# A delta-rule attention feeding a maxout FFN: when weights are converted, four key-query products made and a triangular substitution run inside the first FFN group

## The chip, the cores and the metric

One core of a Trainium2 chip runs the kernel. The metric is the device time in microseconds. Engines are called by the profile's names: PE (TensorE, with PEld for its weight loads), DVE (VectorE), ACT (ScalarE), POOL (GpSimd), SP (SyncE, which here only issues DMAs).

## The reference

```python
# B, H, S, D = 4, 8, 768, 48; d_model = H*D = 384, d_ff = 768
k_n = k / (norm(k, axis=-1, keepdims=True) + 1e-6)
state = zeros((B, H, D, D))
for t in range(S):
    y[:, :, t] = einsum('bhd,bhde->bhe', q[:, :, t], state)
    v_old = einsum('bhde,bhd->bhe', state, k_n[:, :, t])
    state += beta[:, :, t, None, None] * einsum('bhd,bhe->bhde', k_n[:, :, t], v[:, :, t] - v_old)
x = y.transpose(0, 2, 1, 3).reshape(B * S, H * D)        # 3072 x 384
h = maximum(maximum(x @ w1, x @ w2), x @ w3)             # 3072 x 768
out = h @ w_out                                          # 3072 x 384
```

## The kernel before, in words

The recurrence is taken in chunks of 64 positions: 12 chunks, each of two *units* (a unit is half of the batches), so 24 units. Two chunks make a *group*: six groups, each giving 512 rows of x to the FFN. The program is written out by hand (`manual_schedule`): every engine runs its instructions in program order, and each waits only for what it needs.

For a chunk, `gram` makes the key-key products (`at`) and the key-query products (`pt`, masked on DVE by `masked`) of each unit. `to_dram` writes `at` to a DRAM tile, `blocks(m)` reads a group's `at` back with the layout turned, and `solve(m)` runs a forward substitution on DVE: 31 columns of two instructions (L574 makes `tmp`, L578 subtracts it). It is a generator: one step prepares it (norms, scaling), 31 steps are the columns, one step writes the result to DRAM (`y_d`), and two steps issue four reads each from there into `ut`, for the group's first and second chunk. `some(solving, n)` takes n such steps. Then a chunk goes through a chain that `EARLY_LINKS` names by letters:

- z (`join_z`) and j (`join_u`) join the two 32-row halves of `ut`; d (`turn_t1`) transposes parts of it on DVE for j.
- k (`old_k`) and q (`old_q`) multiply by the state; u (`new`), s (`step`, adds to the state on DVE), y (`to_y`, uses `pt`) and x (`to_x`) follow.
- t (`turn`) and g (`gram`) prepare the units of the group after.

Weights come as fp32 bits: `fetch` issues one DMA of 384 KB for a piece, `weights()` converts it: three ACT multiplications (`mant` and two halves of `up`), and a call later `joined` shifts `mant` on DVE (L254) and adds the two on POOL (L263). There are 24 pieces: 18 of w1, w2, w3 (six column blocks, each of the three matrices), then six rows of w_out. For pieces 13 to 21 the kernel before uses another form, two ACT multiplications and one more DVE instruction (L259) that carries the sign. `some(conv, 1)` is one call.

The part in question is the loop over `ffn(0)`, the FFN of group 0, into which the work of groups 1 and 2 is woven. Its 31 steps are:

- 0 to 17: column blocks 0 to 2 of the hidden layer, for 256 rows (0 to 8), then for the other 256 (9 to 17), one weight matrix a step (three pairs of matmuls, 128x256). The first of three steps is copied to `h` by ACT, the two others are maxima on DVE (L949).
- 18 to 26: column blocks 3 to 5 for all 512 rows.
- 27 to 30: the output products with w_out.

The products `p_h` and `p_o` share two PSUM buffers (tag "ffn"), so a step's products wait for the evacuation of the second-last step. All else in PSUM shares three buffers (tag "two"). `at`, `pt`, `h` and a few more share 17 SBUF buffers (tag "square"). The step's products come first; then in this order: fetches, `queries(FIRST[i])`, `links(1, EARLY_LINKS[i])`, the conversion, the substitution, and the rest of the loop (`blocks(2)` at 18, `less_first`, which subtracts w1 from w2 and w3, `turn_first`, `prep_values`, which scales v on POOL by the key norms from `solve`).

In `FIRST` the names T and P are the queries' turns and the key-query products of units 2 to 7: P4 to P7 are four calls of `gram(n, (1,))`, one for each unit of group 1. S takes steps of the substitution of group 1. x and y of that substitution lie inside `wo_sb`, where w_out goes later.

In the profiled execution, step 6 starts on PE at 76.95 us, step 12 at 94.44, step 18 at 111.67, step 20 at 123.89, step 24 at 146.91 and step 27 at 161.57. The FFN of group 1 starts at 179.80.

Of the kernel before, what the change touches and what calls it, by code (L numbers as in the profile page):

```python
# [9 lines left out]
FP32 = mybir.dt.float32  # L10
# [4 lines left out]
ALU = mybir.AluOpType  # L15
# [8 lines left out]
def kernel(  # L24
# [31 lines left out]
    nc = tc.nc  # L56
# [52 lines left out]
    def rows(bb):  # L109
        return slice(C * bb, C * (bb + 1))  # L110
# [19 lines left out]
    def load_k(n, queues=one_queue):  # L130
        load(k, kpad[place(n)], n, queues)

    def load_q(n, queues=one_queue):
        load(q, qpad[n % NQ], n, queues)

    def load_v(c, queue=nc.sync):
        vts[c] = work.tile([128, 2, H, D], FP32, name="v_t", bufs=3)
        for bb in range(2):
            queue.dma_start(  # L139
                out=vts[c][rows(bb)].rearrange("p g h d -> p (g h) d"),  # L140
                in_=v[2 * bb : 2 * bb + 2, :, c * C : (c + 1) * C, :].rearrange(
                    "b h p d -> p (b h) d"
                ),
            )
# [36 lines left out]
    for bb in range(2):  # L181
        nc.gpsimd.affine_select(
            out=mask[rows(bb)], in_=mask[rows(bb)], pattern=[[1, C]], base=-1,
# [4 lines left out]
    t1 = [const.tile([128, 2, H, BL], FP32, name=f"t1{i}") for i in range(NU)]  # L188
# [7 lines left out]
    pieces = []  # L196
# [14 lines left out]
    def fetch(queue=nc.scalar):  # L211
        if fetched[0] < len(pieces):
            _, src, (a, b) = pieces[fetched[0]]
            st = work.tile([128, 2 * 384], U32, name="w_bits", bufs=5)
            queue.dma_start(
                out=st.rearrange("p (a b) -> p a b", a=a), in_=src
            )
            staged.append(st)
            fetched[0] += 1

    def weights():

        waiting = None
        for n, (dst, _, (a, b)) in enumerate(pieces):
            bits = staged.popleft().rearrange("p (a b two) -> p a b two", a=a, two=2)
            low, high = bits[:, :, :, 0], bits[:, :, :, 1]
            mant = work.tile([128, 384], U32, name="mant", bufs=2)
            up = work.tile([128, 384], I32, name="up", bufs=2)  # L230
            mant_v = mant.rearrange("p (a b) -> p a b", a=a)
            up_v = up.rearrange("p (a b) -> p a b", a=a)
            halves = [
                up.bitcast(t)[:, i::2].rearrange("p (a b) -> p a b", a=a)
                for i, t in enumerate((I16, FP16))
            ]

            nc.scalar.mul(mant_v.bitcast(FP32), high.bitcast(FP32), 2.0**-112)
            if not 13 <= n < 22:
                nc.scalar.mul(halves[0], low, 2.0**-29)  # L240
                nc.scalar.mul(halves[1], high.bitcast(FP32), 2.0**-64)
                high = None
            else:
                nc.scalar.mul(up_v, low, 2.0**-29)
            if waiting:
                joined(*waiting)
            waiting = dst, high, mant, mant_v, up_v
            yield
        joined(*waiting)
        yield  # L250

    def joined(dst, high, mant, mant_v, up_v):

        nc.vector.tensor_scalar(  # L254
            out=mant, in0=mant, scalar1=3, scalar2=None,
            op0=ALU.logical_shift_left,
        )
        if high is not None:
            nc.vector.scalar_tensor_tensor(  # L259
                out=mant_v, in0=high, scalar=0x80000000, in1=mant_v,  # L260
                op0=ALU.bitwise_and, op1=ALU.bitwise_or,
            )
        nc.gpsimd.tensor_tensor(  # L263
            out=dst.bitcast(I32), in0=mant_v.bitcast(I32), in1=up_v, op=ALU.add
        )
# [35 lines left out]
    def prep_values(c):  # L301

        if c in nrms:
            scale(c, nrms.pop(c))
# [41 lines left out]
    kqts, ats, pts, xs, at_d = {}, {}, {}, {}, {}  # L346
# [172 lines left out]
    def blocks(m):  # L519
        if m == 1:  # L520
            xs[m] = in_wo(0)
        else:
            xs[m] = work.tile([128, 2, HB * BL + HB], FP32, name="x_bl", bufs=1)
        nc.sync.dma_start(
            out=in_rows(xs[m]),
            in_=at_d[m].rearrange("c f b h j i -> (c f b h) j i"),
        )
# [99 lines left out]
    def both(name, w, bufs=1):  # L627
        return work.tile([128, 2, H, w], FP32, name=name, bufs=bufs)
# [110 lines left out]
    def heads(t):  # L739
        return t.rearrange("p g (j two) d -> p two (g j) d", two=2)  # L740

    def times_state(kqt, i, name):
        p_b = ps_two(name)
        for j in range(NP):
            for g in range(2):
                for par in range(2):
                    for bb in range(2):
                        c0 = (g * NP + j) * D
                        nc.tensor.matmul(  # L749
                            p_b[rows(bb), par, c0 : c0 + D],  # L750
                            kqt[g][dims(par), j, bb ^ g, i],
                            st[dims(par), bb ^ g, g, j],
                        )
        return p_b[:, :, 0 : H * D].rearrange("p two (x d) -> p two x d", d=D)
# [8 lines left out]
            )  # L763

    def old_q(c):
        kqt = [kqts.pop(2 * c + g) for g in range(2)]
        if c:
            qs = qss[c] = both("qs", D)
            nc.scalar.copy(heads(qs), times_state(kqt, 1, "p_q"))
# [211 lines left out]
    def some(gen, n):  # L981
        for _ in range(n):
            if next(gen, gen) is gen:
                break

    conv = weights()
    solving = solve(0)
    zeros(*(t[:, :, :, D:DP] for t in kmore), qall[:, :, :, D:DP])
# [68 lines left out]
    for c in range(2):  # L1057
# [24 lines left out]
    solving = solve(1)  # L1082
# [9 lines left out]
    }  # L1092
    EARLY_LINKS = {
# [3 lines left out]
    }  # L1097


    FIRST = {  # L1100
        0: "f1 s0 T2 S1 S1", 1: "z1 d1 S1 k1 P2 T3 S1 S1", 2: "j1 S1 S1 S1",
        3: "P3 S1 q1 S1 S1", 4: "u1 T4", 5: "y1", 6: "s1 T5 P4", 7: "x1 T6",
        8: "P5 T7", 10: "P6", 12: "P7",
    }


# [8 lines left out]
    def links(m, names):  # L1115
        for name in names.split():
            f, i = name[0], int(name[1])
            if f in RECURS and m < GROUPS:
                RECURS[f](2 * m + i)
            elif f in MADE and m + 1 < GROUPS:  # L1120
                MADE[f](2 * (m + 1) + i)
            elif f in UNIT and m + 1 < GROUPS:
                UNIT[f](4 * (m + 1) + i)
            elif f == "N" and m + 2 < GROUPS:
                load_blocks(4 * (m + 2) + i)

    def queries(names):
        for name in names.split():
            f, n = name[0], int(name[1])
            if f not in OF_KEYS:  # L1130
                links(0, name)
                continue
            OF_KEYS[f](n)
            if f == "T" and n + 3 < 11:
                load_q(n + 3)

    CONVERTED = {*range(9), 10, *range(12, 24)}
    for i, _ in enumerate(ffn(0)):  # L1140
        if i - 1 in CONVERTED:
            fetch(nc.sync)
        queries(FIRST.get(i, ""))
        links(1, EARLY_LINKS.get(i, ""))
        if i in CONVERTED:
            some(conv, 1)
        if 3 < i < 17:
            some(solving, (2, 1, 1, 1, 2, 2, 2, 2, 2, 2, 3, 2, 1)[i - 4])
        if i in (5, 7):
            prep_values(i // 2)  # L1150
        if i in (1, 7):
            for n in range(2):
                load_k(8 + 2 * (i > 1) + n, (nc.gpsimd, nc.gpsimd))
        if i == 0:
            load_v(3)
        if i == 11:
            load_q(11, (nc.gpsimd, nc.gpsimd))
        if i in (10, 22):
            load_v(4 + i // 22)
        if i == 18:  # L1160
            blocks(2)
        if i == 21:
            solving = solve(2)
            some(solving, 1)
        if i == 22:
            prep_values(4)
        if 21 < i < 27:
            some(solving, 3)
        if i >= 27:
            some(solving, 4 if i < 30 else 5)  # L1170
        if i in (27, 28, 29):
            load_blocks(i - 15, nc.sync)
        if i in (15, 17, 19, 22, 25, 27):
            less_first((15, 17, 19, 22, 25, 27).index(i))
        if 27 <= i < 30:
            turn_first((2 * (i - 27), 2 * (i - 27) + 1))
# [5 lines left out]
    for m in range(1, GROUPS):  # L1182
        for i, _ in enumerate(ffn(m)):
# [4 lines left out]
            if m + 2 < GROUPS:  # L1188
                if i == 6:
                    blocks(m + 2)  # L1190
                if i == 8:
                    solving = solve(m + 2)
# [32 lines left out]
```

## Time and profile before

| what | value |
|---|---|
| median of 8 runs | 538.23 us (534.29 to 541.98) |
| the profiled execution | 537.42 us, span 535.7 us |
| mean granted TensorE clock | 0.954 |
| PE busy | 499.7 us (93%) |
| DVE busy | 315.8 us (59%) |
| ACT busy | 160.0 us (30%) |
| POOL busy | 173.8 us (32%) |

The page's shares are means over stages that differ: the first 80 us or so are attention work before and at the start of the FFN, then the FFN of group 0 with the work of groups 1 and 2 in it, then five more FFN groups. In the slices each digit is a fortieth of the span, 13.4 us, in tenths busy; PEclk is the clock granted to TensorE in the same tenths. In a list of waits a row names the waiting instruction, what it waited for, the total in us, the number of waits and the longest. In a timeline a row gives the start, the duration, engine, line, operation and tiles; an idle time ahead of it stands in brackets.

### The profile page before, as it was taken

Reading aid. Unit: us, or ns where it says so; the run is one execution under the profiler, and the core shown is the slowest. Engines: PE = TensorE matmul, PEld = TensorE weight load, DVE = VectorE, ACT = ScalarE, POOL = GpSimd, SP = SyncE. Lnnn points to the kernel's source line nnn. Section 1 sums busy time; section 2 is a strip of 40 time slices with the busy share of each in tenths; the row PEclk is TensorE's granted clock in tenths of the full one; section 3 lists DMA queues with packets and bytes.
Section 4 is the critical chain, followed back from the end, with each engine's and each line's share of the span. In section 5 each row is a group of like instructions: output and inputs, shape, how many; then the busy total and the mean of one; then the engine's idle time right before and its main releaser. Section 6 shows DMA issues by size and latency. Waiting matters only on the chain.

```text
span 535.7 us, 18031 instructions
## 1 busy us (share of the span) xinstructions
PE 499.7 (93%) x7840; PEld 308.8 (58%) x7840; DVE 315.8 (59%) x704; ACT 160.0 (30%) x294; POOL 173.8 (32%) x289
## 2 busy tenths in 40 slices
PE   6657889968899999999999999999999999999996
PEld 5546768834546555556555565565565555654453
DVE  6885989967779553199763699563988222101100
ACT  5547656536222223210134210143101321011100
POOL 7215246322381191694085890411330000000000
PEclk9656989997989999999999999999999999999999
DMA  8876578674123592544394654554334302130011
GB/s 112 185 164 140 104 192 178 131 152 116 32 70 83 112 187 43 127 128 115 84 180 80 158 144 112 118 90 91 89 76 91 64 2 61 45 75 0 0 27 32
DMA packets 114047, 53.45 MB, mean 100 GB/s; under 512 B 95857, under 2 KB 108497, under 8 KB 113969
## 3 DMA queue, kind: packets, MB, share of 16 engines
q1 hardware_dynamic: 104592, 39.02, 33.9%
q0 software_dynamic: 7264, 12.90, 10.1%
q8 instruction: 61, 1.00, 0.8%
q10 hardware_dynamic: 2112, 0.39, 0.5%
q14 instruction: 18, 0.14, 0.1%
HBM read 39.17 MB, written 13.11 MB: 98 GB/s over the span
## 4 chain that ended last, share of the span: by engine, by line
PE 77%; DVE 13%; ACT 3%; issue 2%; DMA 2%; SPq 1%; POOL 0%; DVEq 0%; ACTq 0%; POOLq 0%
PE p_h L935 33%; PE p_o L967 25%; PE p_g L447 3%; PE p_y L819 2%; PE p_m L915 2%; PE p_u L777 2%; PE p_k L749 2%; DVE tmp L574 2%; PE p_q L749 2%; DVE wo_sb L578 2%; PE p_j L732 2%; PE p_s L800 1%; PE p_z L718 1%; DMA kpad<-in_k_dram 1%; ACT ut L593 1%
## 5 line engine op out<-in xcount | busy, mean ns | idle before, releaser
L935 PE MATMUL p_h<-xt,w_sb 128*128 128x512 f32 (+1 forms) x522 | 221.1, 569 | 3.6 <-DVE h L949 1.5
L935 PEld LDWEIGHTS p_h<-xt,w_sb 128*128 128x128 f32 x522 | 96.6, 194 | 90.8 <-issue 82.7
L967 PE MATMUL p_o<-wo_sb,h 128*128 128x384 f32 x288 | 97.8, 489 | 0.0
L949 DVE TENSOR_TENSOR h<-h,p_h 128x512 f32<-128x512 f32 (+1 forms) x48 | 29.6, 616 | 90.8 <-PE p_h L935 90.8
L967 PEld LDWEIGHTS p_o<-wo_sb,h 128*128 128x128 f32 x288 | 53.7, 190 | 35.7 <-issue 0.5
L574 DVE TENSOR_TENSOR tmp<-x_bl,y_bl 128x31 f32<-128x31 f32 (+20 forms) x139 | 52.9, 380 | 4.2
L973 ACT COPY o_sb<-p_o 128x384 f32<-128x384 f32 x24 | 11.5, 479 | 135.6 <-PE p_o L967 129.6
L578 DVE TENSOR_TENSOR y_bl<-y_bl,tmp 128x31 f32<-128x31 f32 (+20 forms) x139 | 47.4, 341 | 4.8
L945 ACT ACTIVATE h<-p_h 128x512 f32<-128x512 f32 x30 | 17.9, 597 | 87.9 <-PE p_h L935 86.4
L967 PE MATMUL p_o<-w_sb,xt 128*128 128x384 f32 x120 | 42.0, 486 | 0.0
L405 POOL DMA_DIRECT2D turned<-in_q_dram x72 | 39.0, 550 | 4.6 <-POOL turned L400 3.0
L447 PE MATMUL p_g<-kqt 48*64 48x64 f32 (+1 forms) x1216 | 28.4, 243 | 7.8 <-DVE nt_bl L272 4.2
L447 PEld LDWEIGHTS p_g<-kqt 48*64 48x64 f32 x1216 | 25.0, 143 | 15.8 <-ACT kqt L376 7.6
L967 PEld LDWEIGHTS p_o<-w_sb,xt 128*128 128x128 f32 x120 | 22.8, 190 | 15.9
L263 POOL TENSOR_TENSOR w_sb<-mant,up 128x384 int32<-128x384 int32 x18 | 18.4, 1023 | 40.3 <-DVE mant L254 26.9
L431 DVE TENSOR_TENSOR pt<-p_g,mask 128x512 f32<-128x512 f32 x22 | 15.1, 688 | 19.7 <-PE p_g L447 15.2
L120 POOL DMA_DIRECT2D kpad<-in_k_dram x32 | 21.8, 688 | 14.7 <-PE p_s L800 14.7
L296 POOL TENSOR_TENSOR v_t<-v_t,nrm 128x768 f32<-128x768 f32 x12 | 18.1, 1510 | 25.5 <-DVE nrm L275 13.5
L807 DVE TENSOR_TENSOR st<-st,p_s 48x768 f32<-48x768 f32 (+1 forms) x18 | 17.1, 949 | 15.4 <-PE p_s L800 15.2
L400 POOL MEMSET turned<- 128x96 f32 x18 | 3.3, 191 | 62.6 <-DVE kqt L421 40.0
L139 POOL DMA_DIRECT2D v_t<-in_v_dram x12 | 9.9, 827 | 36.8 <-PE p_u L777 18.4
L464 ACT COPY at<-p_g 128x512 f32<-128x512 f32 x21 | 12.3, 585 | 29.2 <-DVE pt L431 26.9
(152 smaller groups left out, 611.5 us busy)
## 6 DMA issues: line engine op xcount, KB each, us to landing
w_bits<-in_moe_w_dram SPq DMA_DIRECT2D x18, 384.0 KB
out_dram<-o_sb SPq DMA_DIRECT2D x48, 96.0 KB
turned<-in_q_dram POOLq DMA_DIRECT2D x72, 48.0 KB, 2.6
kpad<-in_k_dram POOLq DMA_DIRECT2D x32, 96.0 KB, 4.7
y_x<-y SPq DMA_DIRECT2D x16, 192.0 KB
qall<-y_x SPq DMA_DIRECT2D x32, 96.0 KB
at_d<-at SPq DMA_DIRECT2D x80, 32.0 KB
ut<-y_d SPq DMA_DIRECT2D x40, 64.0 KB
```

What stands on the lines that cost most here:

```text
L120: queues[bb].dma_start(out=dst[rows(bb ^ g), :, 0:D], in_=src[2 * bb + g, :, c * C : (c + 1) * C, :].rearrange("h p d -> p h d"),)
L263: nc.gpsimd.tensor_tensor(out=dst.bitcast(I32), in0=mant_v.bitcast(I32), in1=up_v, op=ALU.add)
L296: nc.gpsimd.tensor_tensor(out=vts[c], in0=vts[c], in1=nrm[:, :, :, None].to_broadcast([128, 2, H, D]), op=ALU.mult,)
L405: (queue, nc.gpsimd)[i].dma_start(out=t[p0 : p0 + 32, bb, at : at + NP * 2 * D].rearrange("p (j x) -> p j x", j=NP), in_=(k, q)[i][2 * bb ...
L447: nc.tensor.matmul(p_g[rows(bb ^ (g * i)), par, c0 : c0 + C * (1 + whole)], kq[:, 0], kq if whole else kq[:, i],)
L574: nc.vector.tensor_tensor(out=t_v, in0=row.to_broadcast(t_v.shape), in1=column.to_broadcast(t_v.shape), op=ALU.mult,)
L578: nc.vector.tensor_tensor(out=rest, in0=rest, in1=t_v, op=ALU.subtract)
L749: nc.tensor.matmul(p_b[rows(bb), par, c0 : c0 + D], kqt[g][dims(par), j, bb ^ g, i], st[dims(par), bb ^ g, g, j],)
L935: nc.tensor.matmul(p_h, w_sb[i][:, t, f * 128 : (f + 1) * 128], xt[:, t, lo : lo + w], start=(t == 0), stop=(t == KT - 1),)
L945: nc.scalar.activation(out=h, in_=p_h, func=mybir.ActivationFunctionType.Relu)
L949: nc.vector.tensor_tensor(out=h, in0=h, in1=p_h, op=ALU.max)
L967: nc.tensor.matmul(p_o, stays, moves, start=(n == 0), stop=(n == len(terms) - 1))
```

## The change

- `weights()` and `joined()` lose the second form: all 24 pieces are converted with three ACT multiplications, one DVE shift and one POOL addition.
- The calls of the conversion move: steps 0 to 5, 11 to 17 and 20 to 25 (two calls in 22 and 24) instead of 0 to 8, 10 and 12 to 23. The fetches follow them.
- P4 to P7 move from steps 6, 8, 10 and 12 to 14, 15, 16 and 17.
- The substitution of group 1 takes 2, 1, 2, 2, 3, 3, 3, 3, 2, 2 steps in 4 to 13, instead of 2, 1, 1, 1, 2, 2, 2, 2, 2, 2, 3, 2, 1 in 4 to 16. Its last column falls in step 12 instead of 14, with the writes to `y_d`, and all eight reads in 13; before, the writes and the first four reads were in 15 and the last four in 16.
- The links: g0 in 12 (was 13); z0 and z1 in 18 (19); j0 and j1 in 19 (20); u0 in 20 (21); s0 in 21 (22).
- The substitution of group 2 starts in 22 (21), and `prep_values(4)` goes to 23 (22); later steps take five instead of four of its steps.
- `old_q` reads `kqts` without taking the entry out, since P4 to P7 now come after it.

```diff
             nc.scalar.mul(mant_v.bitcast(FP32), high.bitcast(FP32), 2.0**-112)
-            if not 13 <= n < 22:
-                nc.scalar.mul(halves[0], low, 2.0**-29)
-                nc.scalar.mul(halves[1], high.bitcast(FP32), 2.0**-64)
-                high = None
-            else:
-                nc.scalar.mul(up_v, low, 2.0**-29)
+            nc.scalar.mul(halves[0], low, 2.0**-29)
+            nc.scalar.mul(halves[1], high.bitcast(FP32), 2.0**-64)
...
-        if high is not None:
-            nc.vector.scalar_tensor_tensor(
-                out=mant_v, in0=high, scalar=0x80000000, in1=mant_v,
-                op0=ALU.bitwise_and, op1=ALU.bitwise_or,
-            )
...
-        kqt = [kqts.pop(2 * c + g) for g in range(2)]
+        kqt = [kqts[2 * c + g] for g in range(2)]
...
     EARLY_LINKS = {
-        9: "k0 q0", 10: "t0", 11: "t1", 13: "g0 t2", 14: "g1", 15: "t3", 16: "g2", 17: "g3",
-        18: "d0 d1", 19: "z0 z1", 20: "j0 j1", 21: "u0", 22: "s0", 23: "k1 y0 q1",
-        24: "u1 x0", 25: "s1", 26: "y1", 28: "x1",
+        9: "k0 q0", 10: "t0", 11: "t1", 12: "g0", 13: "t2", 14: "g1", 15: "t3",
+        16: "g2", 17: "g3", 18: "d0 d1 z0 z1", 19: "j0 j1", 20: "u0", 21: "s0",
+        23: "k1 y0 q1", 24: "u1 x0", 25: "s1", 26: "y1", 28: "x1",
     }
     FIRST = {
...
-        3: "P3 S1 q1 S1 S1", 4: "u1 T4", 5: "y1", 6: "s1 T5 P4", 7: "x1 T6",
-        8: "P5 T7", 10: "P6", 12: "P7",
+        3: "P3 S1 q1 S1 S1", 4: "u1 T4", 5: "y1", 6: "s1 T5", 7: "x1 T6",
+        8: "T7", 14: "P4", 15: "P5", 16: "P6", 17: "P7",
     }
...
-    CONVERTED = {*range(9), 10, *range(12, 24)}
+    CONVERTED = {i: 1 + (i in (22, 24)) for i in (*range(6), *range(11, 18), *range(20, 26))}
     for i, _ in enumerate(ffn(0)):
-        if i - 1 in CONVERTED:
+        for _ in range(CONVERTED.get(i - 1, 0)):
             fetch(nc.sync)
...
-        if i in CONVERTED:
-            some(conv, 1)
-        if 3 < i < 17:
-            some(solving, (2, 1, 1, 1, 2, 2, 2, 2, 2, 2, 3, 2, 1)[i - 4])
+        some(conv, CONVERTED.get(i, 0))
+        if 3 < i < 14:
+            some(solving, (2, 1, 2, 2, 3, 3, 3, 3, 2, 2)[i - 4])
...
-        if i == 21:
+        if i == 22:
             solving = solve(2)
             some(solving, 1)
-        if i == 22:
+        if i == 23:
             prep_values(4)
-        if 21 < i < 27:
+        if 22 < i < 27:
             some(solving, 3)
         if i >= 27:
-            some(solving, 4 if i < 30 else 5)
+            some(solving, 5)
```

More of the change, by code (lines that the diff above doesn't have):

```diff
@@ L225, in weights @@
         waiting = None
-        for n, (dst, _, (a, b)) in enumerate(pieces):
+        for dst, _, (a, b) in pieces:
             bits = staged.popleft().rearrange("p (a b two) -> p a b two", a=a, two=2)
@@ L238, in weights @@
             nc.scalar.mul(mant_v.bitcast(FP32), high.bitcast(FP32), 2.0**-112)
-            if not 13 <= n < 22:
-                nc.scalar.mul(halves[0], low, 2.0**-29)
-                nc.scalar.mul(halves[1], high.bitcast(FP32), 2.0**-64)
-                high = None
-            else:
-                nc.scalar.mul(up_v, low, 2.0**-29)
+            nc.scalar.mul(halves[0], low, 2.0**-29)
+            nc.scalar.mul(halves[1], high.bitcast(FP32), 2.0**-64)
             if waiting:
                 joined(*waiting)
-            waiting = dst, high, mant, mant_v, up_v
+            waiting = dst, mant, mant_v, up_v
             yield
@@ L250, in weights, with joined @@
         yield
-    def joined(dst, high, mant, mant_v, up_v):
+    def joined(dst, mant, mant_v, up_v):
         nc.vector.tensor_scalar(
```

## The prediction

> **What bounds the kernel now.** First the page's slices: from the twelfth on (about 147 us) TensorE stands at 9 throughout but for the last, at 6. What comes later is paid for in products; idle time to be won lies earlier.
>
> ```profile
> PE   6657889968899999999999999999999999999996
> DVE  6885989967779553199763699563988222101100
> PEclk9656989997989999999999999999999999999999
> ```
>
> The edit first acts in step 6, whose products start at 76.95 us. So next the waits of TensorE alone from 76 to 165 us: four in all.
>
> ```profile
> PE p_z L718 <- DMA ut<-y_d: 4.1, 1, 4.1
> PE p_k L749 <- DVE st L807: 2.6, 1, 2.6
> PE p_h L935 <- DVE h L949: 1.5, 1, 1.5
> PE p_h L935 <- ACT h L943: 0.8, 1, 0.8
> ```
>
> Then the stages of 5 us (span, PE busy, PE loads, VectorE, ScalarE, GpSimd, clock, DMA): two holes, each followed by a low clock.
>
> ```profile
> 115.00:120.00 5.00, 2.74 (x69) 1.21 (x67) 2.20 (x5) 1.45 (x3) 0.54 (x1) 1.00 0.87 163
> 120.00:125.00 5.00, 2.39 (x66) 1.77 (x67) 4.78 (x10) 1.87 (x5) 0.76 (x2) 0.60 0.82 177
> 125.00:130.00 5.00, 5.00 (x135) 2.58 (x133) 4.65 (x8) 3.41 (x7) 2.06 (x2) 0.71 0.43 144
> 140.00:145.00 5.00, 2.44 (x130) 1.91 (x132) 4.83 (x10) 0.25 (x1) 1.55 (x2) 0.99 0.00 0
> 145.00:150.00 5.00, 5.00 (x80) 3.33 (x74) 4.93 (x9) 0.08 (x1) 4.71 (x10) 0.50 0.17 45
> ```
>
> Last the timeline, which says why the first hole is there.
>
> ```profile
> 100.51 0.32 DVE L578 TENSOR_TENSOR wo_sb<-wo_sb,tmp 128x156 f32<-128x156 f32 x1
> 102.77 1.00 POOL L263 TENSOR_TENSOR w_sb<-mant,up 128x384 int32<-128x384 int32 x1 [2.84 <-DVE mant L259]
> 102.86 1.06 DVE L578 TENSOR_TENSOR wo_sb<-wo_sb,tmp 128x135 f32<-128x135 f32 x1
> 108.39 0.21 DVE L578 TENSOR_TENSOR wo_sb<-wo_sb,tmp 128x31 f32<-128x31 f32 x1
> 109.30 1.16 SPq L600 DMA_DIRECT2D y_d<-wo_sb  x2
> 113.16 1.91 SPq L609 DMA_DIRECT2D ut<-y_d  x4
> 115.70 1.86 SPq L477 DMA_DIRECT2D at_d<-at  x4
> 117.66 2.86 SPq L609 DMA_DIRECT2D ut<-y_d  x4
> 121.85 1.27 PE L718 MATMUL p_z<-ut,at 32*32 32x32 f32 x64 [4.11 <-DMA ut<-y_d]
> ```
>
> Group 1's substitution ends at 108.6, its result is written at 109.30, and the second chunk's reads stand on SP behind four `at_d` writes. So z1 (`join_z` of chunk 3) waits. From 80.9 to 109.3 the chain of waits runs through VectorE nearly alone: its queue sets that end. The two L578 rows around 102 us show one of its loads: a column under a GpSimd addition took 1.06, beside 0.32.
>
> **The change part by part.**
>
> *VectorE ahead of the substitution's end.* The four key-query masks (0.69, the next instruction starting 0.60 to 0.68 later) leave steps 6, 8, 10 and 12: 4 x 0.65 = 2.6. Conversions called before the end fall from 13 to 8 (steps 0-8, 10, 12-14 against 0-5, 11, 12): 5 shifts of about 0.3 make 1.5, and four fewer columns under a GpSimd addition, 0.7 each, 2.8. The sign instruction L259 goes: nine of 0.56 (5.0 in all), three ahead of the end, 1.5. Ending in step 12 instead of 14 leaves two maxima (0.37) and one mask (0.6) behind it: 1.3. Sum 9.7, so 98.9. Laid out the other way, VectorE's rows in the new order from 79.7 (17 columns of steps 6-12 at 0.85 falling to 0.35, three maxima, s1's and k0's additions, two shifts, one mask, 2 to 3 us of GpSimd contention), I get 99.5, and take that. The same layout makes step 12's product wait for step 10's maximum: 0.35 us of new TensorE idle. This is the least certain term: 0 to 2.
>
> *TensorE.* P4 to P7 are 4 x 0.63, out of steps 6-12 and into 14-17. All lie before step 18: sum unchanged. Step 18 starts when step 16's maximum is out. VectorE has no columns left in 13-17; its masks, shifts and `less_first` (about 14 us) fit in TensorE's 16. The 1.5 us wait goes: start at 110.6, not 111.67. Gain 1.1.
>
> *SP.* In step 12 a fetch and g0's four `at_d` writes (1.80) stand before the result's two writes: these issue at about 100.8. First reads after 3.85 (109.30 to 113.16): 104.7. Eight reads (1.91 + 2.86) to 109.5, landed 1.3 later (120.52 to 121.85): 110.8. z0 comes at 113.4 behind step 18's product: cover 2.6 us. SP stands still for those 3.85, and queued behind are a fetch a step and g1's, g2's and g3's `at_d` writes. Piece 16, fetched in step 14, goes out at 109.5 and is wanted on ScalarE only after z0. Group 2's `x_bl` read (at 125.18 now) needs those writes, and would go at about 119.5; ScalarE asks for it at 133.
>
> *ScalarE.* Nine pieces take 0.56 + 0.63 + 0.62 instead of 0.56 + 0.55, in queue about 1.55 instead of 1.0: +0.6 each. In 11-17 it has about 18 us for 20; no copy there releases a product sooner than needed. PSUM: eight `two` tiles in steps 14-17 instead of four; each third-last is out 1 us or more ahead. Both at nothing; without that cover about 0.5 a step.
>
> *z and j.* The 17 `square` buffers still run short by two at g3, so its mask on VectorE still waits for z0 (4.46 now); with z in step 18 it waits 3. Behind it on VectorE: shift, `less_first(1)` (1.82), the transposes d0 and d1 (2.7). On ScalarE: at11, a conversion, step 18's h, the four z copies (2.4). From z0's end at 114.1 both chains end near 118.4 for j0 and 119.7 for j1, while step 19's product ends at 117.5. Today step 20's product takes 4.79 at half clock and hides this; now 2.77. New idle 1.5 us in two pieces. Step 18's start to j's end with the three products of 18-20: now 129.99 - 111.67 = 18.3; then 3 x 2.77 + 1.4 (z) + 1.4 (j) + 1.5 = 12.6. Gain 5.7.
>
> *s0 to q1.* s0 in 21 and k1 in 23 have two products between instead of one, and solve(2), whose norm chain (137.32 to 141.57) stands before s0's addition today, starts behind it. Wait of 2.56 gone. From 129.99 to step 24's product at 146.91: 16.9; then 3 x 2.77 + 2 x 1.08 + 3.15 = 13.6. Gain 3.3.
>
> *Steps 24-26.* Step 24's product ran 5.16 at half clock, then 2.77. In exchange solve(2)'s chain (from about 133.6, behind two conversions) pushes k1's subtraction to 140.3, half a us after u1 wants it. 14.7 becomes 13.0. Gain 1.7. The last output weight is added at about 149; its use is at 153: cover 4.
>
> *After that.* solve(2)'s columns would be done at about 172, where SP gets to their write at 173 behind the output writes. Nothing further; TensorE is the bound. On GpSimd the last three additions stand behind `prep_values(4)` (1.47, its norms out at about 136); behind them the issue of group 3's `turned` reads starts at 149 instead of 145.87, for transposes wanted from 171. Fetches that move from steps 7-9 and 11 to 13-23 (384 KB each) find SP free but for the 3.85 above. Keeping `kqts` instead of popping it adds no instruction: unit 4's buffer is read in step 14, and t3's copy in step 15 needs one.
>
> Sum 1.1 + 5.7 + 3.3 + 1.7 = 11.8 us off 537.42 (span 535.7 and 1.7 around it). That run is 0.8 below the median 538.23.
>
> **A rule that speaks against part of it.** The row: an idle of 2.56 us (140.5 to 143.1), then small products, and the clock is 0.50 from about 145 to 151.6. The Trainium skill, "TensorE: Matmul & The Clock Gate", section "Part 1: The HAM clock gate", lets the clock halve after an idle window of about 3.4 us. By it alone this wait is too short to cost clock: the gain of steps 24-26 and of q1 would shrink by about 3, the sum to 8.8. The trace shows that a short idle plus low activity does it, so I count the loss as caused by the wait. The same reading threatens the new idle around j: 1.5 us among 32x32 products. The single 1.5 us at 110 left the clock at 1.00, so I take none there; the other end is 3.3 us, half of such a 6.5 us stretch.
>
> **Rivals.**
> 1. *As above*, 10 to 13 gained: 525 to 528. Chance 0.55.
> 2. *A wait in another's place.* j's idle drops the clock (3.3) and VectorE's backlog in steps 7-12 costs 2 more: 11.8 - 5.3 = 6.5 gained, 531.7. For it: VectorE is 9.6 of 10 busy from 80 to 110, and takes seven steps with 17 columns instead of 14 with six masks and conversions less. Chance 0.25.
> 3. *The reads do not come sooner in effect.* SP's order holds, but the `y_d` landing or reads among w fetches take 5 us longer, z1 waits 2, clock drops, s0's part alone is kept: about 4 gained, 534. Against it: 2.6 us of cover. Chance 0.1.
> 4. *Slower.* Steps 7-12 make TensorE wait about 1 us each, and the clock falls to half for the whole stretch, as in the slices from 30 to 50 us, where PE was 7.2 to 8.3 of 10 busy at 0.50 to 0.53. Some 16 to 18 us of products at half clock add 16 to 18; net of 11.8, about +5: 543. It decides from VectorE needing over some 22.5 us for steps 6-12, against TensorE's 18.1; I count 19.5. Against it: the slice 60-70, 8.84 busy at clock 1.00. Chance 0.1, of which a part ends within 0.5%.
>
> **How the numbers follow.** Likeliest: 538.2 less 11.8, with half a us kept back for what the rows don't show: 527.0. Low end: no j idle, no idle in step 12, u1 unhindered, 2.4 better, and a spread of 1 between runs: 523.5. The high end takes in rivals 2 and 3: 534.5. Half a per cent, about what a measurement of this kernel can tell from no change, is 2.7 us. Faster by more: 0.55 + 0.25 and most of rival 3, 0.87; within: 0.05; slower: 0.08.
>
> **What would show it.** Right: last column near 99 to 100; eight `ut` reads in a row before g1's writes; no wait of z on DMA; k1 without a wait on `st`; clock 1.00 from 115 to 150; output products starting near 150 instead of 161.57. Wrong: waits of p_h on L949 in steps 8-13 summing to over 3 us; clock below 1 before 110; p_j waiting over 2.5 us; p_o waiting on `wo_sb`.

## The result, and the profile after

The changed kernel takes 530.58 us (median of 11 runs, 529.33 to 534.04) against 537.28 us for the kernel before beside it. The ratio is 0.9877, with a 95% interval of 0.9848 to 0.9906: 1.2% faster. The prediction was 527.0, with a range of 523.5 to 534.5. The direction held, and 6.7 us of the forecast 11.2 came.

In the slices, TensorE's 6, 8, 8 from the ninth to the eleventh (107 to 147 us) have become 9, 9, 7; the clock's low digits, the tenth and twelfth before, are now the eleventh and twelfth:

```profile
PE   6557789999799999999999999999999999999996
DVE  5884889863699651399772799553987221111100
PEclk9856999999889999999999999999999999999999
```

The waits of TensorE from 76 to 165 us, in the changed kernel (columns: total, number, longest):

```profile
PE p_u L768 <- DVE v_t L752: 3.3, 1, 3.3
PE p_j L723 <- ACT z L714: 0.7, 2, 0.4
PE p_j L723 <- DVE t L634: 0.6, 1, 0.6
PE p_u L768 <- issue: 0.6, 1, 0.6
```

None of the four waits of before is left. There is the forecast idle around j, 1.4 us in three pieces (0.64, 0.36 and 0.36 in the timeline), and a wait of 3.3 us at u1 that was forecast at half a microsecond. The stages of 5 us (the same columns as before the change) show what it costs:

```profile
115.00:120.00 5.00, 3.64 (x109) 1.88 (x109) 4.81 (x10) 4.79 (x10) 1.18 (x1) 1.00 0.87 199
120.00:125.00 5.00, 4.42 (x118) 2.49 (x104) 1.90 (x5) 2.00 (x4) 0.68 (x1) 1.00 0.59 111
125.00:130.00 5.00, 5.00 (x77) 2.74 (x74) 1.00 (x2) 4.30 (x8) 0.32 (x1) 1.00 0.83 260
140.00:145.00 5.00, 1.72 (x64) 1.72 (x64) 4.93 (x10) 0.82 (x2) 0.50 (x1) 0.73 0.02 3
145.00:150.00 5.00, 5.00 (x24) 2.85 (x16) 3.98 (x9) 5.00 (x10) 3.19 (x4) 0.58 0.00 0
```

The first hole is all but closed, at full clock. Where the second was there is a new one, at 140 us: k1 no longer waits, but u1 does, again with a low clock behind it. The timeline of the part that was rearranged:

```profile
99.42 1.07 DVE L569 TENSOR_TENSOR wo_sb<-wo_sb,tmp 128x31 f32<-128x31 f32 x1
101.53 2.62 SPq L591 DMA_DIRECT2D y_d<-wo_sb  x2
106.10 5.11 SPq L600 DMA_DIRECT2D ut<-y_d  x8
112.00 2.04 SPq L468 DMA_DIRECT2D at_d<-at  x4
113.11 1.35 PE L709 MATMUL p_z<-ut,at 32*32 32x32 f32 x128
143.28 1.96 PE L768 MATMUL p_u<-v_t,ut 64*64 64x48 f32 x64 [3.32 <-DVE v_t L752]
```

The last column ends at 100.5, the eight reads stand in a row ahead of g1's writes, and both z run without a wait.

The table sets all profiles side by side: the time on TensorE from the start of one step's products to the start of another's, and last from step 27 to the start of the FFN of group 1 (the output products). Each ratio is to runs of the kernel before made beside it (medians 536.81 to 538.48), so kernels are compared by their ratios. There is one profile a kernel, and what an edit cannot touch varies between them: a wait near 83 us is 1.1 us long in B3, 1.2 in E7 and absent in the changed kernel, and makes their 33.5 and 33.6. u0 and s0 are in steps 20 and 21 in the changed kernel; in the kernel before, in E3 and in E4 they are one step later, which moves about 1.1 us between the second and third columns.

| run | 6 to 18 | 18 to 21 | 21 to 24 | 24 to 27 | sum | 27 to next FFN | median us | ratio to before |
|---|---|---|---|---|---|---|---|---|
| before | 34.7 | 18.3 | 16.9 | 14.7 | 84.6 | 18.2 | 537.28 | |
| changed | 32.5 | 14.6 | 12.1 | 18.3 | 77.6 | 18.2 | 530.58 | 0.9877 |
| E1 norms behind k1 | 32.9 | 14.7 | 12.1 | 14.9 | 74.6 | 22.9 | 531.84 | 0.9868 |
| E2 one call a step | 32.5 | 13.6 | 12.1 | 13.1 | 71.4 | 19.1 | 527.53 | 0.9792 |
| E3 joins back | 32.5 | 13.7 | 13.4 | 15.7 | 75.3 | 22.1 | 531.90 | 0.9860 |
| E4 columns alone | 37.5 | 14.8 | 18.3 | 14.3 | 84.9 | 18.2 | 538.34 | 1.0003 |
| E5 P4 to P7 back | 33.6 | 17.2 | 12.1 | 17.3 | 80.2 | 18.8 | 531.26 | 0.9883 |
| E6 calls back | 36.8 | 15.3 | 12.2 | 12.7 | 77.0 | 18.2 | 529.56 | 0.9860 |
| E7 old form back | 33.6 | 15.9 | 12.1 | 17.2 | 78.9 | 19.8 | 532.18 | 0.9894 |
| E8 third pair | 32.5 | 13.9 | 12.1 | 13.7 | 72.2 | 22.1 | 528.73 | 0.9849 |
| B2 | 32.5 | 13.6 | 12.2 | 12.6 | 70.9 | 20.1 | 527.74 | 0.9818 |
| B3 | 33.5 | 13.7 | 12.1 | 12.4 | 71.7 | 18.2 | 524.29 | 0.9770 |
| B4 | 32.7 | 12.2 | 12.1 | 12.4 | 69.5 | 20.0 | 524.99 | 0.9788 |

Between the changed kernel and the one before, the stage explains the whole difference of the two profiles: what comes after step 27 took 374.1 us in both (535.7 - 161.57 and 529.5 - 155.43). The stage won 7.1; step 6 happened to start 0.9 later; the spans differ by 6.2. In most of the runs below that is not so: where TensorE reaches the output products before VectorE has made the last maximum, or GpSimd the last weight, part of what was won ahead of step 27 is lost behind it.

### The profile page after: what moved, and what is told of

Its sections match the earlier page's. It is cut to its first block, busy times and chain, and to the rows that moved or that the text cites. A ratio compares the mean times of both kernels' runs of the same rounds, so it can differ in the third digit from the quotient of the medians.

```text
span 529.5 us, 18025 instructions
## 1 busy us (share of the span) xinstructions
PE 495.1 (94%) x7840; PEld 306.6 (58%) x7840; DVE 307.0 (58%) x695; ACT 164.2 (31%) x303; POOL 173.7 (33%) x289
## 4 chain that ended last, share of the span: by engine, by line
PE 77%; DVE 11%; ACT 4%; issue 3%; DMA 2%; SPq 2%; POOL 1%; ACTq 0%; POOLq 0%; DVEq 0%
PE p_h L926 33%; PE p_o L958 25%; PE p_g L438 3%; PE p_u L768 3%; PE p_y L810 2%; PE p_m L906 2%; DVE tmp L565 2%; PE p_j L723 2%; PE p_k L740 2%; SPq L120 2%; PE p_s L791 1%; DVE wo_sb L569 1%; PE p_q L740 1%; PE p_z L709 1%; DMA kmore<-in_k_dram 1%
## 5 line engine op out<-in xcount | busy, mean ns | idle before, releaser
L926 PE MATMUL p_h<-xt,w_sb 128*128 128x512 f32 (+1 forms) x522 | 218.2, 563 | 1.5 <-DVE xt L877 1.3
L569 DVE TENSOR_TENSOR y_bl<-y_bl,tmp 128x31 f32<-128x31 f32 (+20 forms) x139 | 48.8, 351 | 4.8
L438 PE MATMUL p_g<-kqt 48*64 48x64 f32 (+1 forms) x1216 | 27.0, 237 | 7.5 <-DVE nt_bl L263 3.8
L438 PEld LDWEIGHTS p_g<-kqt 48*64 48x64 f32 x1216 | 24.0, 138 | 14.8 <-ACT kqt L367 7.2
L958 PEld LDWEIGHTS p_o<-w_sb,xt 128*128 128x128 f32 x120 | 22.8, 190 | 15.9
L798 DVE TENSOR_TENSOR st<-st,p_s 48x768 f32<-48x768 f32 (+1 forms) x18 | 17.1, 949 | 19.8 <-PE p_s L791 19.6
L768 PEld LDWEIGHTS p_u<-v_t,ut 64*64 64x64 f32 x768 | 14.4, 149 | 14.3 <-issue 9.7
L768 PE MATMUL p_u<-v_t,ut 64*64 64x48 f32 x768 | 16.3, 235 | 5.8 <-DVE v_t L752 3.3
```

The lines of the kernel that those rows point to most:

```text
L438: nc.tensor.matmul(p_g[rows(bb ^ (g * i)), par, c0 : c0 + C * (1 + whole)], kq[:, 0], kq if whole else kq[:, i],)
L569: nc.vector.tensor_tensor(out=rest, in0=rest, in1=t_v, op=ALU.subtract)
L768: nc.tensor.matmul(p_v[rows(bb ^ g), g, i], ut[c % NU][rows(bb), g, h], rhs[rows(bb), g, h],)
L926: nc.tensor.matmul(p_h, w_sb[i][:, t, f * 128 : (f + 1) * 128], xt[:, t, lo : lo + w], start=(t == 0), stop=(t == KT - 1),)
L958: nc.tensor.matmul(p_o, stays, moves, start=(n == 0), stop=(n == len(terms) - 1))
```

## The experiments

### What makes u1 wait

In the changed kernel u1 waits for k1's subtraction on VectorE (L752), which is queued behind the norm chain of group 2's substitution. This is the timeline of that chain, back to what starts it:

```profile
129.00 0.95 DVE L798 TENSOR_TENSOR st<-st,p_s 128x768 f32<-128x768 f32 x1 [4.82 <-PE p_s L791]
129.87 0.35 DVE L250 TENSOR_SCALAR mant<-mant 128x384 uint32<-128x384 uint32 x1
130.37 1.00 POOL L254 TENSOR_TENSOR w_sb<-mant,up 128x384 int32<-128x384 int32 x1 [5.05 <-DVE mant L250]
131.39 0.55 ACT L238 ACTIVATE mant<-w_bits 128x384 f32<-128x384 f32 x1 [1.48 <-POOL w_sb L254]
133.90 0.57 ACT L238 ACTIVATE mant<-w_bits 128x384 f32<-128x384 f32 x1 [0.93 <-POOL wo_sb L254]
136.29 0.25 ACT L261 ACTIVATE root_bl<-x_bl 128x32 f32<-128x32 f32 x1
136.58 0.18 DVE L262 TENSOR_SCALAR nt_bl<-root_bl 128x32 f32<-128x32 f32 x1 [3.58 <-ACT root_bl L261]
139.61 1.23 DVE L551 TENSOR_TENSOR x_bl<-x_bl,bl 128x1024 f32<-128x1024 f32 x1
140.75 1.02 DVE L883 TENSOR_TENSOR w_sb<-w_sb 128x384 f32<-128x384 f32 x2
142.28 0.95 DVE L752 TENSOR_TENSOR v_t<-v_t,p_k 128x768 f32<-128x768 f32 x1
```

Three causes fit: the order on VectorE (theory 1), too much work on ScalarE (theory 2), or, after the first runs, the two buffers of `mant` and `up` (theory 3): both calls of step 22 wait on ScalarE until GpSimd has added an earlier piece. The shift of that piece stands on VectorE behind the state's addition of s0 for the first call, and behind step 22's maximum for the second.

**E1: the norm chain behind k1.**

```diff
-        if i == 22:
+        if i == 23:
             solving = solve(2)
...
-        if i == 23:
+        if i == 24:
             prep_values(4)
-        if 22 < i < 27:
-            some(solving, 3)
+        if 23 < i < 27:
+            some(solving, 4)
```

> The changed kernel with group 2's substitution started in step 23, behind k1's subtraction on VectorE, instead of in step 22 ahead of it (four columns a step in 24 to 26 instead of three; prep_values(4) in 24). If the order on VectorE makes u1 wait (theory 1), the wait of 3.3 us before p_u in step 24 is gone, the clock stays 1.00 from 140 to 150, steps 24 to 26 take about 13 us instead of 18.3, and the kernel runs in about 525.5 us. If u1 is late for another reason, such as ScalarE behind on its conversions (theory 2), the wait stays above 2 us and the time within 2 us of 530.6.

It took 531.84 us (0.9868, interval 0.9824 to 0.9913), no better than the change itself. u1's wait is gone, so the order is indeed what makes it wait, but two other waits came. TensorE's waits in this run, 76 to 175 us:

```profile
PE p_o L958 <- DVE h L940: 3.9, 2, 2.7
PE p_s L791 <- ACT u L773: 1.3, 1, 1.3
```

The chain's 4.2 us, and four columns a step behind it, now stand on VectorE between steps 23 and 26, and the last maxima, which the output products need, are late. The work left the path at one point and came back at the next. Steps 24 to 27 took 14.9, not 13, and the output products 22.9 instead of 18.2: a wait of 2.7 and, behind it, about 3.4 us at a clock of 0.50. The expected time was wrong by 6 us because only the wait taken away was counted.

**E2: one conversion call in each of steps 18 to 25**, instead of two in 22 and 24.

```diff
-    CONVERTED = {i: 1 + (i in (22, 24)) for i in (*range(6), *range(11, 18), *range(20, 26))}
+    CONVERTED = {i: 1 for i in (*range(6), *range(11, 26))}
```

> The changed kernel with one conversion call in each of steps 18 to 25 instead of two in 22 and 24 and none in 18 and 19. Theory 1: the order on VectorE stays, so u1 still waits, but less, since ScalarE reaches the square root of group 2's norms about 2 us sooner: a wait near 1.2 us, some 528 us. Theory 2 (ScalarE's two calls in step 22 are the whole cause): no wait, clock 1.00, about 525.5 us. The extra calls in 18 and 19 may hold u0 by under 1 us.

527.53 us (0.9792, interval 0.9735 to 0.9850). u1 waits 0.8, the clock stays at 1.00 from 90 to 160, and steps 24 to 27 take 13.1. That is theory 1's expectation (a rest of the wait stays), but it doesn't say whether ScalarE's work or its buffers made the double call late.

**E7 and E8 tell these apart.** E7 puts the old form (two ScalarE products and L259) back for pieces 13 to 21, at the new places of the calls:

```diff
-            nc.scalar.mul(halves[0], low, 2.0**-29)
-            nc.scalar.mul(halves[1], high.bitcast(FP32), 2.0**-64)
+            if not 13 <= n < 22:
+                nc.scalar.mul(halves[0], low, 2.0**-29)
+                nc.scalar.mul(halves[1], high.bitcast(FP32), 2.0**-64)
+                high = None
+            else:
+                nc.scalar.mul(up_v, low, 2.0**-29)
...
```

> The changed kernel with the old form (two ScalarE products, one more VectorE instruction) for pieces 13 to 21. In the new place of the calls these pieces are joined from step 15 on, behind the substitution's end, so theory 1 has VectorE's 9 x 0.56 beside other work, and ScalarE 9 x 0.6 lighter: group 2's square root some 1.5 us sooner, u1's wait near 2, 529.5. If the form itself was part of the gain, 532 or more.

532.18 us (0.9894, interval 0.9860 to 0.9929), not distinguishable from the changed kernel. ScalarE had less to do, and the wait did not shrink, against what I expected: TensorE waited 3.4 for u1, and ScalarE only waited longer for GpSimd. (This alone is no proof: L259 is also one more VectorE instruction ahead of GpSimd's addition.) Its waits from 120 to 150 us in E7:

```profile
ACT mant L238 <- POOL w_sb L263: 2.6, 1, 2.6
ACT mant L238 <- POOL wo_sb L263: 1.5, 1, 1.5
```

E8 leaves all work as in the changed kernel and gives the first call of step 22 a third pair of buffers:

```diff
+    def third(n, tag):
+        return dict(tag="o_sb") if n == 19 else dict(tag=tag, bufs=2)
...
-            mant = work.tile([128, 384], U32, name="mant", bufs=2)
-            up = work.tile([128, 384], I32, name="up", bufs=2)
+            mant = work.tile([128, 384], U32, name="mant", **third(n, "mant"))
+            up = work.tile([128, 384], I32, name="up", **third(n, "up"))
```

> The changed kernel with a third pair of buffers (mant, up) for the first conversion call of step 22, taken from the two o_sb buffers that lie idle until step 27; nothing else differs. If that call waits because both mant buffers are held until GpSimd has added, and that addition stands behind the state's addition of s0 on VectorE (theory 3), ScalarE does it 1.5 us sooner and group 2's square root comes at about 134.2 instead of 136.3 (step 6 at 77.9): u1's wait falls from 3.3 to about 1.2, some 528 us. If ScalarE's own work is the cause (theory 2), root and wait stay: 530.6. Old form for nine pieces, which made ScalarE lighter, left the wait at 3.4, which speaks for theory 3.

528.73 us (0.9849, interval 0.9809 to 0.9890). In its timeline the calls follow each other, and the square root comes 55.1 us after step 6's start instead of 58.4. Of these 3.3 us, 2.5 lie behind step 21's start, about the two waits that went (1.48 and 0.93); the rest is a shorter stage around j, which the edit does not touch. The rows are the starts of step 22's two calls and the root:

```profile
128.24 0.54 ACT L241 ACTIVATE mant<-w_bits 128x384 f32<-128x384 f32 x1
129.87 0.55 ACT L241 ACTIVATE mant<-w_bits 128x384 f32<-128x384 f32 x1
132.25 0.25 ACT L264 ACTIVATE root_bl<-x_bl 128x32 f32<-128x32 f32 x1
```

u1's wait fell to 1.4 us, without a low clock behind it. But most of what the stage won (72.2 instead of 77.6) is lost again behind it: step 27's last products wait for the last maximum, the clock falls, and the output products take 22.1 us instead of 18.2. The wait, and one microsecond of the stretch behind it (span, PE busy, clock, DMA share, GB/s):

```profile
PE p_o L961 <- DVE h L943: 1.9, 1, 1.9
157.00:158.00 1.00, 1.00 (x3) 0.50 0.54 117
```

The intervals of E8 and of the changed kernel overlap in the total, so the proof lies in ScalarE's waits, u1's wait and the stage (13.7 instead of 18.3), not in the time. It settles theory 3 for the late start of the chain; E1 shows theory 1, why a late chain reaches TensorE.

### Which parts of the change carry the gain

**E4: the columns' new pace alone**, on the kernel before.

```diff
-        if 3 < i < 17:
-            some(solving, (2, 1, 1, 1, 2, 2, 2, 2, 2, 2, 3, 2, 1)[i - 4])
+        if 3 < i < 14:
+            some(solving, (2, 1, 2, 2, 3, 3, 3, 3, 2, 2)[i - 4])
```

> The kernel before, with only the pace of group 1's substitution taken from the change (last column in step 12, reads in 13); conversions, P4 to P7 and joins as before. If VectorE's queue is the bound, the substitution ends near 106 instead of 108.6, TensorE waits 2 to 4 us on maxima in steps 9 to 13, z1 no longer waits on its reads, and about 3 us are gained: 534. If the order on SP alone makes the difference, the gain is 6 us or more. k1's wait on the state stays at 2.6 us.

538.34 us (1.0003, interval 0.9981 to 1.0024): nothing gained. z1's wait on the reads did go. But VectorE, not relieved, held up TensorE in steps 9 and 13. TensorE's waits from 75 to 165 us, and a stage with a low clock:

```profile
PE p_k L749 <- DVE st L807: 3.6, 1, 3.6
PE p_h L935 <- POOL wo_sb L263: 2.3, 1, 2.3
PE p_h L935 <- DVE h L949: 1.4, 1, 1.4
PE p_q L749 <- DVE pt L431: 1.3, 1, 1.3
90.00:95.00 5.00, 4.96 (x50) 0.75 1.20 199
```

Steps 6 to 18 took 37.5 instead of 34.7, which with k1's wait (3.6 here; 1.4 more in 21 to 24) used up the 3.5 won in 18 to 21. The 2.3 is a wait that was not expected: step 20's product needs the buffer that ScalarE's copy of step 18's h frees, and that copy ended at 122.09, 0.15 us ahead of the product. It stands on ScalarE behind g3's copy to `at`, which waited for g3's mask, and that for z. (The list names GpSimd, whose addition merely ended last.) The expected 534 left out this wait and the clock.

**E5: P4 to P7 back in steps 6, 8, 10 and 12.**

```diff
-        3: "P3 S1 q1 S1 S1", 4: "u1 T4", 5: "y1", 6: "s1 T5", 7: "x1 T6",
-        8: "T7", 14: "P4", 15: "P5", 16: "P6", 17: "P7",
+        3: "P3 S1 q1 S1 S1", 4: "u1 T4", 5: "y1", 6: "s1 T5 P4", 7: "x1 T6",
+        8: "P5 T7", 10: "P6", 12: "P7",
```

> The changed kernel with P4 to P7 back in steps 6, 8, 10 and 12. If VectorE's queue ahead of the substitution's end is what counts (theory 1), their four masks put 2.6 us back there: the last column ends near 103 instead of 100.5 (step 6 starting at 77.9), TensorE waits about 2 us on maxima in steps 7 to 13, the reads land near 115, z0 waits 1 us: 533. If only the order on SP counts (theory 2), the time stays at 530.6.

531.26 us (0.9883, interval 0.9834 to 0.9931), the same as the change. The last column ended 25.9 us after step 6's start instead of 22.6, 3.2 later where 2.6 was expected; but TensorE waited only 0.3 on maxima, and z not at all. (The longer steps 18 to 21 in the profile, 17.2, are a stretch of low clock behind j, for which see the end.) So the four masks are relief that the other parts made unnecessary. The expectation of 533 was too high.

**E6: the conversion calls back in the steps of before**, in the new form.

```diff
-    CONVERTED = {i: 1 + (i in (22, 24)) for i in (*range(6), *range(11, 18), *range(20, 26))}
+    CONVERTED = {i: 1 for i in (*range(9), 10, *range(12, 24))}
```

> The changed kernel with its conversion calls in the steps of the kernel before (0 to 8, 10, 12 to 23), all in the new form. Theory 1: five shifts and four columns held up by GpSimd's additions return ahead of the substitution's end, 4.3 us, which ends near 105; maxima are late in steps 8 to 13 and z waits about 3 us, while ScalarE has only one call in step 22, so u1 waits about 1 us instead of 3.3. Net some 2 us slower: 532.5. Theory 2: only the one call in 22 is felt, 528.5.

529.56 us (0.9860, interval 0.9822 to 0.9899). Steps 6 to 18 lost 4.3 (36.8 against 32.5), all of it waits, and steps 24 to 27 won 5.6. The last column ended 26.1 us after step 6's start, 3.5 later, where 4.3 of shifts and contention were expected; that TensorE lost the same 4.3 is chance. TensorE's waits, 75 to 185 us:

```profile
PE p_h L926 <- DVE h L940: 2.8, 3, 1.6
PE p_t L361 <- DVE v_t L752: 1.5, 1, 1.5
PE p_u L768 <- DVE v_t L752: 0.4, 1, 0.4
```

So in these profiles moving the calls was worth 4.3 us, and placing them two to a step in 22 gave it back. z did not wait here as I had expected, since TensorE itself reached it 4 us later.

**E3: the joins back** in steps 19 to 22.

```diff
-        16: "g2", 17: "g3", 18: "d0 d1 z0 z1", 19: "j0 j1", 20: "u0", 21: "s0",
+        16: "g2", 17: "g3", 18: "d0 d1", 19: "z0 z1", 20: "j0 j1", 21: "u0", 22: "s0",
```

> The changed kernel with z, j, u0 and s0 back in steps 19, 20, 21 and 22 (d stays in 18). If the joins' earlier place brings part of the gain, z or k1 gets a wait and the time rises by 2 us or more. If the gain is that the reads land before z and that VectorE is free for s0 (my steps), the idle of 1.4 us around j goes, nothing else comes, and the time is 1 us lower or the same: 529 to 531. u1's wait stays at about 3 us, as group 2's substitution still starts ahead of k1.

531.90 us (0.9860, interval 0.9807 to 0.9914): no loss. The idle around j went, and k1 did not wait; instead step 20 waited 2.8 for ScalarE's copy of step 18's h, which in the kernel before too waited for z. Steps 6 to 27 took 2.3 less than in the changed kernel, and the output products 3.9 more (a wait of 2.0 on the last maximum, and a low clock). As placed, the joins' earlier steps are worth nothing measurable. That k1 is free even with s0 in step 22 points to the later start of group 2's norm chain, which no longer stands ahead of s0's addition; this was not tried alone.

In their total times E3, E5, E6 and E7 cannot be told from the changed kernel. What each part is worth is therefore read from waits and steps of single profiles; in the time itself only the whole change is shown.

### Better versions

**B2**: E2's calls, and `less_first` in 15, 19, 21, 23, 25, 27.

```diff
-        if i in (15, 17, 19, 22, 25, 27):
-            less_first((15, 17, 19, 22, 25, 27).index(i))
+        if i in (15, 19, 21, 23, 25, 27):
+            less_first((15, 19, 21, 23, 25, 27).index(i))
```

> One conversion call a step in 18 to 25 (as in the faster run so far), and less_first in 15, 19, 21, 23, 25, 27 instead of 15, 17, 19, 22, 25, 27, so that it stands neither ahead of d0 and d1 nor ahead of k1's subtraction on VectorE. Theory 1: u1's wait of 0.8 goes and j's idle stays bound by ScalarE's z copies; about 1 us lower than 527.5: 526.5. If VectorE has no slack in 23 to 26, maxima get late for the output products and nothing is gained: 527.5 or more.

527.74 us (0.9818, interval 0.9780 to 0.9855). u1's wait went to 0.2, and p_o waited 1.6 on the last maximum instead: no gain over E2.

**B3**: B2 with two columns a step in 23 to 26 and six in 27 to 30.

```diff
-            some(solving, 3)
+            some(solving, 2)
         if i >= 27:
-            some(solving, 5)
+            some(solving, 6)
```

> One call a step in 18 to 25, less_first in 15, 19, 21, 23, 25, 27, and two columns of group 2's substitution a step in 23 to 26 with six in 27 to 30 instead of three and five. If what is left in steps 24 to 27 is VectorE's backlog, the wait of p_o on the last maximum (1.6) goes and the kernel takes 526. If the columns moved into 27 to 30 no longer fit there (six of 0.85 against a step of 5.2), group 2's result is written late and z in the next FFN group waits: 529.

524.29 us (0.9770, interval 0.9728 to 0.9812), the fastest by its median, and clear of the changed kernel's interval, though not of E2's. The output products are back at 18.2. TensorE's waits, 75 to 185 us, are these three:

```profile
PE p_h L926 <- DVE h L940: 1.1, 1, 1.1
PE p_j L723 <- ACT z L714: 0.7, 2, 0.4
PE p_j L723 <- ACT z L712: 0.3, 1, 0.3
```

**B4**: B3 with the call of step 17 moved to the end.

```diff
+    CONVERTED = {i: 1 for i in (*range(6), *range(11, 17), *range(18, 27))}
```

> As the run with two and six columns, and the conversion call of step 17 moved to the end (calls in 0 to 5, 11 to 16, 18 to 26), so that ScalarE reaches step 18's copy and the z copies about 1.5 us sooner. Theory 1 and the sum on record: j's idle of 1.1 us goes: 525. If the last weight, now joined in step 26, is late for the output products, p_o waits on it and it is 527 or more.

524.99 us (0.9788, interval 0.9746 to 0.9829), the same as B3. j's idle went, and p_o waited 1.5 us on the last weight, as the second half of the expectation has it.

## Why the prediction was right or wrong, point by point

- *VectorE ahead of the substitution's end.* From step 6's start to the last column's end: 31.65 us before, 22.62 after, 9.0 less, against 9.7 by the sum and 9.1 by the layout that was taken. E5 and E6 bear out two of its terms (3.2 back for the masks, against 2.6, and 3.5 for the calls, against 4.3). The new idle at step 12 was 0.09 and not 0.35, with 0.08 more at step 9.
- *TensorE, steps 6 to 18.* Gained 2.2 instead of 1.1: the wait of 1.5 went, and the stage's own work was shorter than my sum (32.5; P4 and g1, for one, ran as 96 matmuls in 1.68 us).
- *SP.* The writes issued at 101.5, the reads from 106.1 to 111.2: 0.7, 1.4 and 1.7 us later than on the sheet, 0.9 of it because step 6 itself started later. The cover held, and z did not wait; but with the sheet's 1.3 us to land, only about 0.6 of the 2.6 us was left (an estimate from these rows).
- *z and j.* From step 18 to the end of step 20's product 12.77 us, where 12.6 were predicted; idle of 1.36, in three pieces, against 1.5 in two.
- *s0 to q1.* 14.0 against 13.6, with a wait of 0.57 at u0 that was not seen.
- *Steps 24 to 26: the step that failed.* The text had solve(2)'s chain start "from about 133.6, behind two conversions" and u1 late by half a microsecond, a gain of 1.7. The square root came at 136.29, u1 waited 3.32, and the clock fell: p_u, p_x and step 25's product took 7.2 us to their ends instead of 4.65. The stage took 18.3 and not 13.0, and the output products started at 155.43, not near 150. The 5.3 us are 2.8 of wait and 2.5 of clock, and they are more than the whole miss of 4.7 us: 2.2 + 5.5 + 2.9 - 3.6 = 7.0 measured (7.1 unrounded) against 11.8, with steps 6 to 18 1.1 better than forecast. Of the 2.8, 1.8 is the chain's late start (133.6 on the sheet is 134.5 with step 6 0.9 later, against 136.29); most of the rest is that TensorE wanted u1 about 0.7 sooner than the sheet had it.
- The cause inside that step is that the two conversions were costed by ScalarE's own time, 1.55 each. I had bounded PSUM's buffers, but not the two buffers of `mant` and `up`, whose release runs over VectorE and GpSimd. E8 shows it: with the buffers' wait gone, u1 waits 1.4 instead of 3.3.
- *Nothing further after step 27.* Right to within 0.1 us.
- *The rivals.* What came has the size of the second (6.5), by another mechanism: not the backlog in steps 7 to 12, where TensorE waited 0.2 us, but a queue some 15 steps later. That 530.6 lies within the stated range is therefore in part luck: its upper part was meant for the second and third rivals, and neither happened. (The second rival sets 17 columns in seven steps against 14 before; by the change as listed it was 12 before.) E4 shows that the fourth rival's mechanism exists: with VectorE not relieved, those steps do hold up TensorE and cost clock, though it cost a draw and not 5 us.

## What to carry to other kernels

When two calls of a small pipeline are put into one slot, cost its buffers and not only its engines: follow who frees the buffer, and what stands ahead of that instruction on its own queue. A long chain in an in-order queue belongs behind the short instruction that the critical engine waits for, but moving it only pays if the queue has room where it lands (E1, B2, then B3). And a gain in idle time is safe only when every other engine in the stage is relieved as well: the same columns, moved without relief, gave nothing.

## What was not expected of the hardware

The clock after an idle time cannot be read from its length in these runs. In the one profile of each kernel, idle times on TensorE of 4.1 and 2.6 us (before), 3.3 (changed), 1.9 (E8) and 1.3 (E4) were followed by half speed, at the latest 2 us after the idle's end. Others were not: 1.6 in E6, 1.3 in E7, 2.8 in E3, and in E3 also 3.4, the changed kernel's wait at the same place. There the clock stayed at 1.00:

```profile
140.00:145.00 5.00, 1.87 (x71) 1.00 0.02 3
145.00:150.00 5.00, 5.00 (x75) 1.00 0.00 0
```

In E5 only 1.7 us, in three pieces between the 32x32 products of j, and the clock was at 0.50 for 7 us; the changed kernel had 1.4 us there and kept 1.00.

```profile
115.00:120.00 5.00, 3.35 (x131) 0.83 0.96 245
120.00:125.00 5.00, 5.00 (x10) 0.50 0.46 121
```

The Trainium skill ("TensorE: Matmul & The Clock Gate", section "Part 1: The HAM clock gate") calls the window of activity free-running, which would make the phase decide. That would fit what is seen, though no run here shows the window itself. Its idle length of about 3.4 us does not fit: in E4 an idle of 1.3 us was followed by half speed, in E8 one of 1.9. Half-speed stretches lasted from about 3.4 us (E6, 125 to 129) to 7 us. So my prediction's reading, that the wait itself causes the loss, was too firm: in these runs an idle of 1 to 4 us brings a chance of losing about 1.7 to 3.5 us more (half of such a stretch).
